# A 2048-point column transform split as 128 x 16 in place of 16 x 128, real and imaginary parts packed in one tile

## The chip, the cores and the metric

The kernel runs on one core of a Trainium2 chip. The core has five engines: TensorE (PE in the profile; its weight loads are PEld), VectorE (DVE), ScalarE (ACT), GpSimd (POOL) and SyncE (SP), which here issues DMAs. The metric is the device time of one execution in microseconds (us), as a median of runs.

## What is computed

The input x is 2048 x 640 in fp32. Two branches are mixed by a gate for each row. Cut to what matters:

```python
g = sigmoid((x * gate_w).sum(-1))                 # one number per row
# A: attention of each row to itself and 7 earlier rows, 2 apart; 32 heads of 20
q, k, v = split(x @ wqkv)                         # 640 x 1920
attn = softmax(where(idx >= 0, q.k * 20**-0.5, -1e9))
a = (attn @ v) @ wo                               # 640 x 640
# B: a filter in the frequency domain
X = rfft2(x)                                      # over 2048 rows and 640 columns
b = irfft2(X * (w_r + 1j * w_i), (2048, 640))
out = g * a + (1 - g) * b
```

The change concerns branch B alone. Its two-dimensional transform consists of a transform over the 640 columns (here: the row transform, within each row) and one over the 2048 rows (the column transform), forward and back. All of it is done with matmuls against tables of sines and cosines.

## The kernel before

**Layout.** Row s = 16 p + j of x lies in partition p of tile j, j = 0 to 15. Even j ("par 0") and odd j ("par 1") are handled apart for the attention, since a row attends only to rows of its own parity.

**The order of the work.** The program does not issue instructions as it is written. Every call is recorded by `Plan.record` (lines 174 to 190) with what it reads and writes and with a cost from `Plan.cost` (line 192 on), and `Plan.order` (lines 226 to 291) then lays out one fixed list for each engine: at each step the engine takes, of the operations that are ready by the planned times, the one with the longest chain of planned work behind it (its `tail`). Chains with a name ("logits", "sums", "even") count the rest of their own chain on an engine in that tail. All instructions of the trace therefore carry one line, L460, and are told apart by their tiles. On the chip each engine runs its list strictly in order; a SyncE DMA that waits for a buffer holds up the DMAs behind it.

**The stages** (`work`, line 392):

1. `qkv` (512), up to 237.8 us: x @ wqkv for the even rows, then the odd rows, each product split in three matmuls of a shorter fp32 format (tiles xe and xo by w). Results go to DRAM through `ev`.
2. `fold` (624) and `cols` (647), inside stage 1: each row is folded by its symmetries (f), and the matmul `z <- fc, f` does the first part of the column transform: a 16-point real transform over groups of 16 partitions (`fc` is a 128 x 128 table, eight copies of it interleaved). ScalarE copies z to `zg`, the big intermediate (128 partitions, 5 blocks, 128 positions, 16 components).
3. `attend` (550), from about 80 us to 456: for each half of four heads, VectorE forms the products pr of q and k and sums them to the logits L, GpSimd, ScalarE and VectorE do the softmax, GpSimd multiplies by v (pv, two operations at a time), VectorE sums to o (o0a to o7b), and o is stored in DRAM (od). It is spread over VectorE and GpSimd beside all other stages. The two last halves, 4a and 4b, are done in lockstep in four pieces, so that rows become complete one pair of tiles after the other.
4. `freq` (669), from 237.8 us to about 366: the rest of the transform, the filter and the way back, for one frequency kk of the 16-point transform at a time, in the order KORD (line 20), staged four deep. Seven are full (two components, real and imaginary), and kk = 0 and 8 are half (one real component). For a full one:
   - ScalarE copies its two components out of zg (`zc`, 640 elements at a stride of 16); SyncE loads the tables `md` and `mf` and the weights `wp`.
   - TensorE does the row transform: `u` and `v`, three matmuls each (widths 321, 161, 160) for each component; ScalarE copies v to `vs`; VectorE makes four sums `ab` of 321 elements.
   - TensorE does the 128-point complex column transform: `xa`, `xb` (the rows k) and `xc`, `xd` (the mirrored rows), two matmuls of 321 columns each.
   - The filter: ScalarE copies xa and xb to `X`, GpSimd multiplies by wp to `P`, twice 642 elements and then two sums; VectorE takes xc and xd straight from PSUM, with four products (`p`, and in place), two sums, and four sums of P with them to `s`, the stationary operands of the inverse.
   - The inverse column transform: `g <- mf, s`, for each of 5 blocks two matmuls of 256 columns that add up (one term from s1, one from s2). ScalarE copies g back into zg.
   A half frequency leaves out half of this; its sums run on GpSimd and ScalarE, and its g matmuls have 128 columns.
5. `project_even` (872): for each even j, the o rows are loaded (`ot`), transposed by TensorE (`oTp`), split (`oT`), multiplied by wo (`woa`, `wob`, 15 matmuls each), scaled by the gate and stored (`ad`). They have no early deadline and fill TensorE from about 300 us on.
6. `spatial` (797), 366 to 440 us: `oa`, `ob` (inverse row transform, six matmuls), copies `os`, then `ha`, `hb <- os, fct`: the last 16-point inverse. Odd j: ScalarE scales into `ho`. Even j: VectorE combines (tiles h, ha, y), GpSimd adds the even projection (yi), and the row is stored.
7. `project_odd` (888), 440 us to the end: as 5, for odd j, with the final sum on VectorE.

**Buffers around the change.** PSUM has eight banks. `freq` uses one for v, two for u, two in turn for xa to xd, one for g (line 29). In SBUF zc, md, wp, ab, P, s and X have two buffers each, vs, p and mf one (lines 374 to 376). Tags are shared between stages: the tile x7, last used by stage 1, is also the oT of `project_even` (line 379), and a later user of a tag waits for all earlier ones.

Of the kernel before, what the change touches and what calls it, by code (L numbers as in the profile page):

```python
# [16 lines left out]
S, D = 2048, 640  # L17
NJ = 16
HD = 20
KORD = (0, 8, 1, 2, 3, 4, 5, 6, 7)  # L20
# [12 lines left out]
def dft_tables():  # L33
    tau = 2 * np.pi
    ke, ko = PERM[:161], PERM[161:]
    kb = PERM[2:161]
    b = np.arange(16)
    coef = np.zeros((16, 16))
    coef[0] = 1
    coef[1] = (-1.0) ** b  # L40
    for k in range(1, 8):
        coef[2 * k] = np.cos(tau * b * k / 16)
        coef[2 * k + 1] = -np.sin(tau * b * k / 16)
    fc = np.einsum("cb,ae->baec", coef, np.eye(8)).reshape(128, 128)
# [15 lines left out]
    a = np.arange(128)  # L60
    a = 16 * (a % 8) + a // 8
    k1 = np.arange(128)
    md = np.zeros((9, 128, 384))
    mf = np.zeros((9, 128, 512))
    for kk in range(9):
        psi = tau * (np.outer(k1, a) / 128 + kk * a[None, :] / 2048)
        c, s = np.cos(psi), np.sin(psi)
        md[kk] = np.concatenate([c.T, s.T, -s.T], 1)
        mf[kk] = np.stack([np.stack([c, s], 2), np.stack([s, -c], 2)], 1).reshape(128, 512)
# [3 lines left out]
    def ck(k):  # L73
# [12 lines left out]
        "t_fc": np.concatenate([fc, fc.T], 1).astype(f),  # L86
        "t_bt": bt.astype(f),
        "t_md": md.astype(f),
        "t_mf": mf.astype(f),
# [240 lines left out]
class Mixer:  # L330
# [17 lines left out]
    def places(self, pp, dr, sb):  # L348
# [8 lines left out]
        self.ident, self.fc, self.fct = (self.one(n, 128) for n in ("ident", "fc", "fct"))  # L357
# [34 lines left out]
    def work(self):  # L392
# [25 lines left out]
        self.zg = self.one("zg", 5, 128, 16, tag="big")  # L418
# [11 lines left out]
        S.dma_start(self.fct, ins["t_fc"][:, 128:256])  # L430
# [11 lines left out]
        freq = [self.freq(kk) for kk in KORD]  # L442
# [204 lines left out]
    def cols(self, q):  # L647
        p = self.p
        f = self.folded[q]
        for t0, n in ((0, 2), (2, 2), (4, 1)):  # L650
            z = self.ps(BP, f"z{q}_{t0}")
            for i in range(2 * n):
                t, j = t0 + i // 2, i % 2
                p.pe.matmul(
                    z[:, i * 128 : i * 128 + 128],
                    f[:, j, t * 128 : t * 128 + 128],
                    self.fc,
                    start=(i == 0),
                    stop=(i == 2 * n - 1),
                    skip_group_check=True,  # L660
                )
            p.chain = "z"
            p.act.copy(
                self.zg[:, t0 : t0 + n, 16 * q : 16 * q + 16, :].rearrange("p t a c -> p t (a c)"),
                z[:, 0 : 256 * n].rearrange("p (t m) -> p t m", t=n),
            )
            p.chain = ""

    def freq(self, kk):
# [3 lines left out]
        full = kk not in (0, 8)  # L673
        comps = (2 * kk, 2 * kk + 1) if full else ((0,) if kk == 0 else (1,))
        pm = 2 if full else 1
        md, wp = self.mdr.next(f"md{kk}", 384), self.wpr.next(f"wp{kk}", 4, 321)
        S.dma_start(md, ins["t_md"][kk])
        S.dma_start(wp[:, 0 : 2 * pm], ins["ws"][kk, :, 0 : 2 * pm])

        us, vs, zcs = {}, {}, {}  # L680
        for c in comps:
            zcs[c] = self.zcr.next(f"zc{c}", 5, 128)
            A.copy(zcs[c], zg[:, :, :, c])

        def row(o, c, t, r, start, stop):
            T.matmul(o, zcs[c][:, t], r, start=start, stop=stop, skip_group_check=True)

        if full:
            vv = self.vsr.next(f"vs{kk}", 2, 321)
        for c, d in zip(comps[::-1], comps):  # L690
            v = self.ps(BV, f"v{c}")[:, 0:321]
            row(v, c, 3, bt[:, 803:1124], True, False)
            row(v[:, 0:161], c, 2, bt[:, 642:803], False, False)
            row(v[:, 161:321], c, 4, bt[:, 1124:1284], False, True)
            if full:
                A.copy(vv[:, c % 2], v)
                v = vv[:, c % 2]
            u = self.ps(BU, f"u{d}")[:, 0:321]
            row(u, d, 1, bt[:, 161:482], True, False)
            row(u[:, 0:161], d, 0, bt[:, 0:161], False, False)  # L700
            row(u[:, 161:321], d, 2, bt[:, 482:642], False, True)
            us[d], vs[c] = u, v
        us, vs = [us[c] for c in comps], [vs[c] for c in comps]

        ab = self.abr.next(f"ab{kk}", 4, 321)
        if full:
            v0, v1 = vs
            V.tensor_sub(ab[:, 0], us[0], v1)
            V.tensor_add(ab[:, 2], us[0], v1)
            V.tensor_add(ab[:, 1], us[1], v0)  # L710
            V.tensor_sub(ab[:, 3], v0, us[1])
        else:
            A.copy(ab[:, 1], vs[0])
            A.copy(ab[:, 0], us[0])

        yield
        cs, sn, ns = md[:, 0:128], md[:, 128:256], md[:, 256:384]

        def col(nm, i, sa, sb):
            o = self.ps(BX, f"{nm}{kk}")[:, 0:321]  # L720
            T.matmul(o, sa, ab[:, i], start=True, stop=False)
            T.matmul(o, sb, ab[:, i + 1], start=False, stop=True)
            return o

        x0, x1 = col("xa", 0, cs, sn), col("xb", 0, ns, cs)
        X = self.Xr.next(f"X{kk}", 2, 321)
        A.copy(X[:, 0], x0)
        A.copy(X[:, 1], x1)
        P = self.Pr.next(f"P{kk}", 4, 321)
        G.tensor_mul(P[:, 0:2], X, wp[:, 0:2])  # L730
        G.tensor_mul(P[:, 2:4], X, wp[:, 1::-1])
        if full:
            G.tensor_sub(P[:, 0], P[:, 0], P[:, 1])
            G.tensor_add(P[:, 2], P[:, 2], P[:, 3])

        yield
        mf = self.mfr.next(f"mf{kk}", 512)
        S.dma_start(mf, ins["t_mf"][kk])
        s12 = self.s12r.next(f"s{kk}", 2, 640)
        s1, s2 = s12[:, 0], s12[:, 1]  # L740
        if full:
            x2, x3 = col("xc", 2, cs, ns), col("xd", 2, sn, cs)
            t = self.p1r.next(f"p{kk}", 2, 321)
            V.tensor_mul(t[:, 0], x2, wp[:, 2])
            V.tensor_mul(x2, x2, wp[:, 3])
            V.tensor_mul(t[:, 1], x3, wp[:, 2])
            V.tensor_mul(x3, x3, wp[:, 3])
            V.tensor_sub(x3, t[:, 0], x3)
            V.tensor_add(x2, t[:, 1], x2)
            V.tensor_add(s1[:, 0:321], P[:, 0], x3)  # L750
            V.tensor_sub(s2[:, 321:640], P[:, 0, 2:], x3[:, 2:])
            V.tensor_add(s1[:, 321:640], P[:, 2, 2:], x2[:, 2:])
            V.tensor_sub(s2[:, 0:321], x2, P[:, 2])
        else:
            G.tensor_sub(s1[:, 0:321], P[:, 0], P[:, 1])
            G.tensor_sub(s2[:, 321:640], P[:, 0, 2:], P[:, 1, 2:])
            G.tensor_add(s1[:, 321:640], P[:, 2, 2:], P[:, 3, 2:])
            G.tensor_add(P[:, 0], P[:, 2], P[:, 3])
            A.mul(s2[:, 0:321], P[:, 0], -1.0)
        yield  # L760
        n = 256 if full else 128
        per = 2 if full else 4
        m1 = mf[:, 0:256] if full else mf[:, 0:256:2]
        m2 = mf[:, 256:512] if full else mf[:, 256:512:2]
        for t0 in range(0, 5, per):
            k = min(per, 5 - t0)
            g = self.ps(BG, f"g{kk}_{t0}")
            for i in range(k):
                t = t0 + i
                go = g[:, i * n : i * n + n]  # L770
                T.matmul(go, s1[:, t * 128 : t * 128 + 128], m1, start=(i == 0), stop=False, skip_group_check=True)
                T.matmul(go, s2[:, t * 128 : t * 128 + 128], m2, start=False, stop=(i == k - 1), skip_group_check=True)
            if full:
                A.copy(
                    zg[:, t0 : t0 + k, :, 2 * kk : 2 * kk + 2].rearrange("p t a r -> p (t a) r"),
                    g[:, 0 : k * n].rearrange("p (t r) -> p t r", r=2),
                )
            else:
                A.copy(zg[:, t0 : t0 + k, :, comps[0]].rearrange("p t a -> p (t a)"), g[:, 0 : k * n])
# [17 lines left out]
    def spatial(self, j):  # L797
# [21 lines left out]
        T.matmul(h1[:, 0:322], self.fct, os[:, 0:322], start=True, stop=True)  # L819
        T.matmul(h2[:, 0:322], self.fct, os[:, 322:644], start=True, stop=True)  # L820
# [117 lines left out]

def arrays_of(inputs):
# [4 lines left out]
    up = [16 * np.arange(128) + k for k in range(9)]  # L944
    down = [(2048 - r) % 2048 for r in up]
# [29 lines left out]
```

## Time and profile before

| | |
|---|---|
| median of 3 runs | 484.64 us (484.53 to 484.76) |
| profiled execution | 485.85 us, span of its instructions 484.1 us |
| TensorE, its weight loads | 474.5 us busy (98% of the span), 406.2 (84%) |
| VectorE, GpSimd, ScalarE | 405.3 (84%), 372.2 (77%), 235.2 (49%) |
| DMA moved | 101.59 MB, mean 210 GB/s |
| granted TensorE clock | 1.00 throughout |

How to read the lines that follow: a row of a group names the engine, the operation, the tile written and the tiles read ("g<-mf,s"; buffer numbers are left out), the shape and the count; then the busy time of the group and the mean ns of one; then the idle time of the engine just before these instructions and who ended it. An fp32 matmul appears as two MATMUL records with a weight load each, so 10 calls are 20 records. Rows of the chain in order of time have start, length, engine and tile, and a count of records. Rows of waits have the total in us, the number of times and the longest. Rows by stage have, behind the stretch's ends and its length, the busy time of each engine with its number of instructions, then the granted clock, the DMA share and GB/s. In a timeline a row has start and length.

### The profile page before, as it was taken

What the parts mean: (1) busy time and instruction counts of PE and PEld (TensorE: products, weight loads), DVE (VectorE), ACT (ScalarE), POOL (GpSimd) and SP (SyncE); (2) the same over time, 40 slices, a digit from 0 to 9 for tenths busy, and PEclk for the clock granted to TensorE, in tenths of its full rate; (3) what the DMA queues carried; (4) which work ended last, traced back from release to release, by engine and by line L of the source; (5) the groups of instructions that cost most, each with busy time, mean ns of one, the idle gap of its engine ahead of it and who ended that gap; (6) DMA issues with size and microseconds to landing.
All of it is one profiled execution on the core that took longest, in us unless ns stands there. A gap on an engine that the chain in (4) does not pass through costs nothing.

```text
span 484.1 us, 7137 instructions
## 1 busy us (share of the span) xinstructions
PE 474.5 (98%) x2449; PEld 406.2 (84%) x2449; DVE 405.3 (84%) x511; ACT 235.2 (49%) x474; POOL 372.2 (77%) x316
## 2 busy tenths in 40 slices
PE   8999999999999999999999999999999999998997
PEld 5888888888898898888878777888878888887996
DVE  4989789947999999896983778989999998879536
ACT  5633456733375654674496445355344755433110
POOL 1014437989999899896999777787688989799990
PEclk9999999999999999999999999999999999999999
DMA  8999999797787895987674433744544322345752
GB/s 280 401 401 317 405 301 323 214 340 194 228 264 246 245 325 145 262 235 197 222 238 125 164 108 109 245 132 137 172 118 128 89 71 73 120 159 160 255 164 82
DMA packets 77460, 101.59 MB, mean 210 GB/s; under 512 B 21344, under 2 KB 58848, under 8 KB 77424
## 3 DMA queue, kind: packets, MB, share of 16 engines
q1 hardware_dynamic: 51136, 80.91, 52.9%
q10 hardware_dynamic: 25376, 16.22, 10.8%
q0 software_dynamic: 912, 4.00, 2.0%
q8 instruction: 19, 0.31, 0.2%
q14 instruction: 17, 0.14, 0.1%
HBM read 68.28 MB, written 32.84 MB: 209 GB/s over the span
## 4 chain that ended last, share of the span: by engine, by line
PE 93%; DMA 3%; DVE 2%; ACT 1%; issue 1%; DVEq 0%
PE qkv L460 43%; PE woa L460 7%; PE wob L460 7%; PE g L460 7%; PE ob L460 4%; PE oa L460 4%; PE z L460 3%; PE v L460 3%; PE u L460 3%; PE xb L460 2%; PE ha L460 2%; PE oTp L460 2%; PE hb L460 2%; PE xa L460 2%; PE xd L460 1%; PE xc L460 1%
## 5 line engine op out<-in xcount | busy, mean ns | idle before, releaser
L460 PE MATMUL qkv<-w,xo 128*128 128x480 f32 (+1 forms) x480 | 106.2, 382 | 0.5 <-ACT zg L460 0.5
L460 PEld LDWEIGHTS qkv<-w,xo 128*128 128x128 f32 x480 | 90.2, 189 | 15.0 <-ACT zg L460 0.7
L460 PE MATMUL qkv<-w,xe 128*128 128x480 f32 (+1 forms) x465 | 102.5, 382 | 0.0
L460 PEld LDWEIGHTS qkv<-w,xe 128*128 128x128 f32 x465 | 87.6, 188 | 14.8 <-ACT w L460 0.2
L460 ACT COPY ev<-qkv 128x480 f32<-128x480 f32 x64 | 35.6, 561 | 57.7 <-PE qkv L460 39.0
L460 PE MATMUL woa<-wo,oT 128*128 128x320 f32 x240 | 54.3, 318 | 0.6 <-ACT oT L460 0.6
L460 PE MATMUL wob<-wo,oT 128*128 128x320 f32 x240 | 53.8, 316 | 0.6 <-ACT ya L460 0.6
L460 PEld LDWEIGHTS wob<-wo,oT 128*128 128x128 f32 x240 | 40.1, 188 | 1.9 <-ACT ya L460 0.9
L460 PEld LDWEIGHTS woa<-wo,oT 128*128 128x128 f32 x240 | 40.0, 188 | 1.9 <-ACT oT L460 0.8
L460 PE MATMUL g<-mf,s 128*128 128x256 f32 (+1 forms) x180 | 39.9, 359 | 0.6 <-ACT zg L460 0.4
L460 POOL TENSOR_TENSOR w<-raw,w 128x480 fp32r<-128x480 f32 (+1 forms) x20 | 25.3, 1278 | 15.4 <-ACT w L460 15.4
L460 PEld LDWEIGHTS g<-mf,s 128*128 128x128 f32 x180 | 30.7, 189 | 7.5 <-ACT zg L460 2.6
L460 POOL DMA_DIRECT2D fd<-fx x6 | 4.3, 722 | 37.2 <-DVE fx L460 35.3
L460 POOL TENSOR_TENSOR P<-X,wp 128x642 f32<-128x642 f32 x18 | 26.6, 1503 | 6.9 <-ACT X L460 6.9
L460 ACT CAST oT<-oTp 128x384 fp32r<-128x384 f32 (+1 forms) x32 | 13.1, 430 | 28.9 <-PE oTp L460 28.9
L460 DVE TENSOR_TENSOR oT<-oTp,oT 128x384 fp32r<-128x384 f32 (+1 forms) x32 | 15.0, 485 | 11.5 <-ACT oT L460 11.3
L460 ACT COPY zg<-g 128x512 f32<-128x512 f32 (+2 forms) x25 | 14.0, 560 | 19.6 <-PE g L460 19.5
L460 PE MATMUL oa<-gt,zg 128*128 128x161 f32 (+1 forms) x96 | 22.0, 344 | 0.0
L460 ACT COPY zc<-zg 128x640 f32<-128x640 f32 x16 | 20.6, 1323 | 1.2 <-PE u L460 1.2
L460 PE MATMUL v<-bt,zc 128*128 128x321 f32 (+2 forms) x96 | 20.6, 345 | 0.6 <-ACT zc L460 0.6
L460 PE MATMUL ob<-gt,zg 128*128 128x161 f32 (+1 forms) x96 | 21.0, 344 | 0.0
L460 PE MATMUL u<-bt,zc 128*128 128x321 f32 (+2 forms) x96 | 20.6, 344 | 0.0
(316 smaller groups left out, 1147.0 us busy)
## 6 DMA issues: line engine op xcount, KB each, us to landing
qkvd<-ev ACTq DMA_DIRECT2D x32, 480.0 KB, 4.6
raw<-in_wqkv SPq DMA_DIRECT2D x25, 240.0 KB, 6.1
fx<-in_x SPq DMA_DIRECT2D x8, 641.0 KB, 9.3
ot<-od SPq DMA_DIRECT2D x16, 320.0 KB, 3.1
wp<-in_ws SPq DMA_DIRECT2D x7, 642.0 KB, 4.1
fd<-fx POOLq DMA_DIRECT2D x6, 640.0 KB, 8.1
f<-fd SPq DMA_DIRECT2D x6, 640.0 KB, 5.3
xt<-in_xT SPq DMA_DIRECT2D x8, 320.0 KB, 4.0
```

The source lines that it names most:

```text
L460: p.dve.memset(w, 0.0)
```

## The change

The 2048-point column transform is split the other way round. `fc` becomes a real transform over the 128 partitions: 64 frequencies with real and imaginary part fill the 128 outputs (frequency 64, which is real, takes the place of the imaginary part of frequency 0). What remains is a 16-point complex transform over j, done for 16 groups of four of these frequencies: the 128 partitions of a group are 2 parts x 16 j x 4 frequencies. Group 0 holds the two special frequencies and has tables of its own.

- `zg` is (128, 5, 16 j, 128); `zc` is made by three ScalarE operations: 3 blocks as they are, and 3 blocks with real and imaginary parts exchanged and a sign (so that v comes out multiplied by the imaginary unit).
- u and v have three matmuls each for each of 16 groups, as they had for each of 16 components; `ab` takes two VectorE sums.
- xa, xb, xc and xd are one matmul of 321 columns each (two in group 0).
- GpSimd does one product of 642 and one sum to P; VectorE three operations on xc and xd and two to s.
- The inverse g is one matmul of 128 columns for each of 5 blocks (six in group 0), in tiles of three and two blocks.
- `wp` has 16 tiles of 4 x 321 (before: 7, and two of 2 x 321); the tables are five tiles of 3 x 320 in the place of the nine md and nine mf, and 1280 elements for group 0, in the tile x7.
- `fct` is two tables of 128 x 128, and ha and hb are two matmuls of 161 columns each, in place of one of 322.
- The order of the groups is 1, 2, 3, 0, 4 to 15. The other stages, the planner and its costs are unchanged.

The diff's core (for `freq`, the added and kept lines; the removed ones stand in the listing above; the loops that fill the sine tables of the groups are left out):

```diff
-KORD = (0, 8, 1, 2, 3, 4, 5, 6, 7)
+GORD = (1, 2, 3, 0) + tuple(range(4, 16))
...
+    pos = np.arange(128)
+    fc = np.zeros((128, 16, 2, 4))
+    for k in range(64):
+        fc[:, k // 4, 0, k % 4] = np.cos(tau * pos * k / 128)
+        fc[:, k // 4, 1, k % 4] = -np.sin(tau * pos * k / 128)
+    fc[:, 0, 1, 0] = (-1.0) ** pos
+    back = np.stack([fc, np.stack([-fc[:, :, 1], fc[:, :, 0]], 2)]).reshape(2, 128, 128)
+    fc = fc.reshape(128, 128)
...
-        self.zg = self.one("zg", 5, 128, 16, tag="big")
+        self.zg = self.one("zg", 5, NJ, 128, tag="big")
...
-    def freq(self, kk):
+    def freq(self, g):
         p, ins = self.p, self.ins
         V, A, G, T, S = p.dve, p.act, p.pool, p.pe, p.sp
         zg, bt = self.zg, self.bt
+        if g == 0:
+            tb = self.one("tbfirst", 1280, tag="x7")
+            S.dma_start(tb, ins["t_first"])
         else:
+            if g % 3 == 1:
+                self.mm = self.mdr.next(f"mm{g}", 3, 320)
+                S.dma_start(self.mm, ins["t_mm"][(g - 1) // 3])
+            tb = self.mm[:, (g - 1) % 3]
+        wp = self.wpr.next(f"wp{g}", 4, 321)
+        S.dma_start(wp, ins["ws"][g])
+        zc = self.zcr.next(f"zc{g}", 6, NJ, 8)
+        A.copy(zc[:, 0:3], zg[:, 0:3, :, 8 * g : 8 * g + 8])
+        A.mul(zc[:, 3:6, :, 0:4], zg[:, 2:5, :, 8 * g + 4 : 8 * g + 8], -1.0)
+        A.copy(zc[:, 3:6, :, 4:8], zg[:, 2:5, :, 8 * g : 8 * g + 4])
+        def row(o, t, r, start, stop):
+            T.matmul(o, zc[:, t].rearrange("p j c -> p (j c)"), r, start=start, stop=stop, skip_group_check=True)
+        v = self.ps(BV, f"v{g}")[:, 0:321]
+        row(v, 4, bt[:, 803:1124], True, False)
+        row(v[:, 0:161], 3, bt[:, 642:803], False, False)
+        row(v[:, 161:321], 5, bt[:, 1124:1284], False, True)
+        vv = self.vsr.next(f"vs{g}", 321)
+        A.copy(vv, v)
+        u = self.ps(BU, f"u{g}")[:, 0:321]
+        row(u, 1, bt[:, 161:482], True, False)
+        row(u[:, 0:161], 0, bt[:, 0:161], False, False)
+        row(u[:, 161:321], 2, bt[:, 482:642], False, True)
+        ab = self.abr.next(f"ab{g}", 2, 321)
+        V.tensor_add(ab[:, 0], u, vv)
+        V.tensor_sub(ab[:, 1], u, vv)
         yield
+        def col(nm, i, turned):
+            o = self.ps(BX, f"{nm}{g}")[:, 0:321]
+            if g == 0:
+                c = 256 * i + 128 * turned
+                T.matmul(o, tb[:, c : c + 128], ab[:, 0], start=True, stop=False)
+                T.matmul(o, tb[:, 512 + c : 640 + c], ab[:, 1], start=False, stop=True)
+            else:
+                c = 0 if turned else 64
+                T.matmul(o, tb[:, c : c + 128], ab[:, i], start=True, stop=True)
             return o
+        X = self.Xr.next(f"X{g}", 2, 321)
+        for i, nm in enumerate(("xa", "xb")):
+            A.copy(X[:, i], col(nm, 0, i))
+        P = self.Pr.next(f"P{g}", 2, 321)
+        G.tensor_mul(P, X, wp[:, 0:2])
+        G.tensor_add(P[:, 0], P[:, 0], P[:, 1])
         yield
+        z, sz = col("xc", 1, 0), col("xd", 1, 1)
+        t = self.p1r.next(f"p{g}", 321)
+        V.tensor_mul(t, z, wp[:, 2])
+        V.tensor_mul(sz, sz, wp[:, 3])
+        V.tensor_sub(sz, t, sz)
+        s = self.s12r.next(f"s{g}", 768)
+        d0 = 321
+        if g == 0:
+            d0 = 449
+            G.memset(s[:, 384:449], 0.0)
+        V.tensor_add(s[:, 0:321], P[:, 0], sz)
+        V.tensor_sub(s[:, d0 : d0 + 319], P[:, 0, 2:], sz[:, 2:])
         yield
+        last = s[:, 640:768] if g == 0 else s[:, 512:640]
+        chunks = [[(s[:, 0:128], 0)], [(s[:, 128:256], 0)], [(s[:, 256:384], 0)], [(s[:, 384:512], 1)], [(last, 1)]]
+        if g == 0:
+            chunks[2:4] = [[(s[:, 384:512], 1), (s[:, 256:321], 0)], [(s[:, 512:640], 1)]]
+        for t0, n in ((0, 3), (3, 2)):
+            o = self.ps(BG, f"g{g}_{t0}")
+            for i in range(n):
+                for w, back in chunks[t0 + i]:
+                    m = tb[:, 1024 + 128 * back : 1152 + 128 * back] if g == 0 else tb[:, 192:320]
+                    T.matmul(
+                        o[0 : w.shape[1], i * 128 : i * 128 + 128],
+                        w,
+                        m,
+                        start=(i == 0),
+                        stop=(i == n - 1),
+                        skip_group_check=True,
+                    )
+            A.copy(
+                zg[:, t0 : t0 + n, :, 8 * g : 8 * g + 8],
+                o[:, 0 : n * 128].rearrange("p (t j c) -> p t j c", t=n, c=8),
+            )
...
-            st = zg[:, t, 8 * j : 8 * j + 8, :].rearrange("p a c -> p (a c)")
-            T.matmul(o, st, r, start=start, stop=stop, skip_group_check=True)
+            T.matmul(o, zg[:, t, j], r, start=start, stop=stop, skip_group_check=True)
...
-        T.matmul(h1[:, 0:322], self.fct, os[:, 0:322], start=True, stop=True)
-        T.matmul(h2[:, 0:322], self.fct, os[:, 322:644], start=True, stop=True)
+        for i, h in enumerate((h1, h2)):
+            for a in range(2):
+                T.matmul(
+                    h[:, 161 * a : 161 * a + 161],
+                    self.fct[:, a],
+                    os[:, 322 * i + 161 * a : 322 * i + 161 * a + 161],
+                    start=(a == 0),
+                    stop=(a == 1),
+                    skip_group_check=True,
+                )
...
+def rows_of(g):
+    up = np.tile((4 * g + np.arange(4)[None] + 128 * np.arange(16)[:, None])[None], (2, 1, 1))
+    if g == 0:
+        up[:, :, 0] = [0, *range(128, 1024, 128), *range(64, 1088, 128)]
+        up[1, 0, 0] = 1024
+    down = (2048 - up) % 2048
+    return up.reshape(-1), down.reshape(-1)
```

More of the change, by code (lines that the diff above doesn't have):

```diff
@@ L58, in dft_tables @@
     )
[L60 to L69, printed above, removed]
+    j, k2 = np.arange(16), np.arange(16)
+    md = np.zeros((16, 16, 2, 4, 2, 16, 4))
@@ new lines, in dft_tables @@
+    mf = np.zeros((16, 2, 16, 4, 16, 2, 4))
+    for g in range(16):
+        for a in range(4):
+            th = tau * np.outer(j, 4 * g + a + 128 * k2) / 2048
+            c, s = np.cos(th), np.sin(th)
+            md[g, :, 0, a, 0, :, a], md[g, :, 1, a, 0, :, a] = c, s
+            md[g, :, 0, a, 1, :, a], md[g, :, 1, a, 1, :, a] = -s, c
+            mf[g, 0, :, a, :, 0, a], mf[g, 1, :, a, :, 0, a] = c.T, -s.T
+            mf[g, 0, :, a, :, 1, a], mf[g, 1, :, a, :, 1, a] = s.T, c.T
+    u0, u64, v0, v64 = (np.zeros((2, 2)) for _ in range(4))
@@ new lines, in dft_tables @@
+    first = np.zeros((2, 2, 2, 16, 2, 4, 2, 16, 4))
+    g0 = md[0].copy()
+    g0[:, :, 0] = 0
+    for x in range(2):
+        first[x, x, 0] = g0
+        first[x, x, 1, :, :, :, 0], first[x, x, 1, :, :, :, 1] = -g0[:, :, :, 1], g0[:, :, :, 0]
+    first[:, :, :, :, :, 0, :, :, 0] = one
+    first = first.reshape(8, 128, 128).transpose(1, 0, 2).reshape(128, 1024)
+    mfu, mfv = mf[0].copy(), mf[0].copy()
+    for q, w in ((mfu, mu), (mfv, mv)):
+        q[:, :, 0] = 0
+        q[:, :, 0, :, :, 0] = w
@@ L85, in dft_tables @@
     return {
[L86 removed]
+        "t_fc": np.concatenate([fc, back[0].T, back[1].T], 1).astype(f),
         "t_bt": bt.astype(f),
[L88 to L89 removed]
+        "t_mm": mm.reshape(5, 3, 128, 320).transpose(0, 2, 1, 3).astype(f),
+        "t_first": first.astype(f),
         "t_gt": gt.astype(f),
@@ L356, in places @@
         self.a_d = dr.tile([128, 8, D], F32, tag="dram_a", name="ad")
-        self.ident, self.fc, self.fct = (self.one(n, 128) for n in ("ident", "fc", "fct"))
+        self.ident, self.fc = (self.one(n, 128) for n in ("ident", "fc"))
+        self.fct = self.one("fct", 2, 128)
         self.z, self.g, self.ng, self.nng = (self.one(n, NJ) for n in ("z", "g", "ng", "nng"))
@@ L672, in freq @@
         zg, bt = self.zg, self.bt
[L673 to L702, printed above, removed]
@@ L719, in col @@
[L719 to L722, printed above, removed]
-            return o
[L725 to L731, printed above, removed]
@@ L952, in arrays_of @@
         "wo": wo.reshape(5, 128, D),
-        "ws": np.stack([np.stack([w[r][:, PERM] for r in (up[k], down[k]) for w in (wr, wi)], 1) for k in range(9)]),
+        "ws": np.stack([np.stack([w[r][:, PERM] for r in rows_of(g) for w in (wr, wi)], 1) for g in range(16)]),
     }
```

97 lines of the change are left out of this document (28 added, 69 removed).

## The prediction

> **What bounds the kernel now.** First the page: busy times and the engines of the chain that ended last.
>
> ```profile
> span 484.1 us, 7137 instructions
> ...
> PE 474.5 (98%) x2449; PEld 406.2 (84%) x2449; DVE 405.3 (84%) x511; ACT 235.2 (49%) x474; POOL 372.2 (77%) x316
> ...
> PE 93%; DMA 3%; DVE 2%; ACT 1%; issue 1%; DVEq 0%
> ```
>
> TensorE is busy for 98% of the span and 93% of the final chain. The whole is an average, so next come the busy times by stage: frequency groups (237.8 to about 366), spatial transform and even projections (to 440), odd projections (to the end). A first row holds the columns; the last row, from a second question, runs to the moment at which the first pieces of the last attention halves (4a, 4b) exist.
>
> ```profile
> core 0: us, PE busy (x) PEld busy (x) DVE busy (x) ACT busy (x) POOL busy (x), PEclk, DMA share, GB/s
> 237.80:297.00 59.20, 58.11 (x285) 46.07 (x285) 40.84 (x69) 35.19 (x64) 50.07 (x46) 1.00 0.54 170
> 297.00:412.00 115.00, 113.85 (x610) 96.50 (x609) 108.53 (x134) 60.16 (x124) 96.03 (x74) 1.00 0.42 125
> 412.00:440.00 28.00, 27.70 (x148) 22.68 (x146) 24.29 (x51) 11.52 (x28) 25.35 (x21) 1.00 0.40 126
> 440.00:484.10 44.10, 39.70 (x278) 38.99 (x276) 26.46 (x53) 6.22 (x16) 29.88 (x36) 1.00 0.55 178
> ...
> 237.80:427.90 190.10, 187.86 (x983) 156.26 (x983) 161.94 (x228) 102.28 (x202) 159.35 (x132) 1.00 0.46 140
> ```
>
> Two things stand here. From 237.8 to 440, TensorE is idle for only 2.5 us (1.09 + 1.15 + 0.30), so work taken from it there should shorten the span. But VectorE is close behind: 108.53 of 115 us from 297 to 412, because the attention runs beside the transforms. If TensorE gets shorter, VectorE may become the bound. So I make two sums, one for each engine.
>
> **TensorE's sum.** An fp32 matmul shows as two records. Their spacing is the price, not their duration (records overlap), and the chain in order of time gives it: start, length, records.
>
> ```profile
> 138.90 4.46 PE z L460 x40
> 237.80 1.09 PE v L460 x6
> 272.25 1.73 PE g L460 x8
> 273.98 1.08 PE xc L460 x4
> 324.33 2.20 PE woa L460 x15
> 370.59 0.54 PE ha L460 x2
> 383.43 0.55 PE ob L460 x4
> ```
>
> A record takes 0.1115 us at 128 columns (z), 0.1375 at 161 (ob), 0.216 at 256 (g), 0.27 at 321 (xc, ha). Now the counts.
>
> ```profile
> L460 PE MATMUL g<-mf,s 128*128 128x256 f32 x140 | 34.5, 382 | 0.5 <-ACT zg L460 0.4 <-issue 0.2
> L460 PE MATMUL g<-mf,s 128*128 128x128 f32 x40 | 5.5, 277 | 0.1
> L460 PE MATMUL xa<-ab,md 128*128 128x321 f32 x36 | 11.8, 440 | 0.0
> L460 PE MATMUL xc<-ab,md 128*128 128x321 f32 x28 | 9.2, 433 | 0.0
> ```
>
> *Inverse (g).* Before: 140 records of 256 columns and 40 of 128, 140 x 0.216 + 40 x 0.1115 = 34.7 us. After: 16 groups of 5 matmuls and one extra for group 0, 81 matmuls or 162 records of 128 columns: 18.1 us. Saved: 16.7. This is "the inverse in one term": real and imaginary parts fill the 128 partitions, so one matmul does what two did. *Forward columns (xa to xd).* Before: 2 x 36 + 2 x 28 = 128 records. After: 15 groups of 4 matmuls and group 0 with 8, 68 matmuls, 136 records: +8 x 0.27 = +2.2 us. *ha and hb.* 32 matmuls of 322 columns become 64 of 161: 128 x 0.1375 - 64 x 0.27 = +0.3 us. *Rows (u, v) and z* keep their number and widths: nothing. Net: -14.2 us. All these widths are priced by rows above; none is extrapolated.
>
> The change also adds weight loads: 180 + 128 + 64 = 372 before, 162 + 136 + 128 = 426 after, 54 more. The z row shows that one load per 128-column record hides: its 0.1115 us is the streaming rate of the 256-column row, halved (0.108), plus 0.0035. So I charge nothing more. The Trainium skill (Perfetto Trace Analysis, "Identifying the Most-Contended Engine") speaks against this reading: it says to judge TensorE by the busy share of weight loads and not by that of matmuls, and that share (84%) would rise here. What this would give is a rival below.
>
> **VectorE's sum, and the other engines.**
>
> ```profile
> L460 DVE TENSOR_TENSOR p<-xd,wp 128x321 f32<-128x321 f32 x7 | 3.4, 492 | 5.5 <-PE xd L460 5.3
> L460 POOL TENSOR_TENSOR P<-X,wp 128x642 f32<-128x642 f32 x18 | 26.6, 1503 | 6.9 <-ACT X L460 6.9
> L460 POOL TENSOR_TENSOR P<-P 128x321 f32<-128x321 f32 x16 | 11.8, 758 | 0.2
> L460 POOL TENSOR_TENSOR s<-P 128x319 f32<-128x319 f32 x4 | 3.0, 750 | 0.0
> L460 ACT COPY zc<-zg 128x640 f32<-128x640 f32 x16 | 20.6, 1323 | 1.2 <-PE u L460 1.2
> L460 ACT COPY X<-xb 128x321 f32<-128x321 f32 x9 | 3.9, 429 | 6.7 <-PE xb L460 6.6
> wp<-in_ws SPq DMA_DIRECT2D x7, 642.0 KB, 4.1
> ```
>
> *VectorE.* Before: 14 operations of about 321 elements in each of seven full frequencies, none in the other two: 98. After: 7 in each of 16 groups: 112. The 14 more cost 14 x 0.48 = +6.7 us (the row: 0.49, the second term of s a little less). *GpSimd.* Before: 18 x 1.50 + 16 x 0.76 + 6 x 0.75 (four in the row, two of 321) = 43.7. After: 16 x (1.50 + 0.76) = 36.2 and one small memset (under 0.75, the nearest row): -7. *ScalarE.* zc's one strided copy of 640 becomes three of 384, 192 and 192 in runs of 8 or 4 elements. At the strided price of 2.07 ns an element, the 768 elements cost 1.6 us a group, 25.4 in all; at the price of the X copy (1.34 ns) 1.0, 16.4. So -4 to +5 beside 20.6. The v and X copies go from 14 and 18, with four copies to ab, to 16 and 32: +12 x 0.43 = 5. ScalarE has half its time free: on the path, nothing. *DMA.* 16 weight tiles of 642 KB take the place of seven and two halves, eight more, in all some 4 MB with the smaller tables; at a DMA share of about 0.5 I charge nothing while the second buffer of wp (4.1 us to land) covers it. The SP queue issues 22 loads for the groups where it issued 27; each wp waits there for VectorE's last use of the buffer two groups back, with the attention's loads and stores behind it. That wait existed; it now comes 14 times in place of 7, and what it costs is in the bounds below, through the attention.
>
> What decides is when the last attention halves are far enough for the odd projections. The timelines of VectorE and of TensorE, then the landing times of o4b's stores and of ot's loads:
>
> ```profile
> 426.41 1.49 DVE L460 TENSOR_REDUCE o4b<-pv4b 128x160 f32<-128x1280 f32 x1 [2.53 <-POOL pv4b L460]
> ```
>
> ```profile
> 437.83 0.38 PE L460 MATMUL oTp<-ident,ot 128*128 128x128 f32 x2
> ```
>
> ```profile
> DMA to landing us min/median/max: 1.7/2.1/5.4
> ```
>
> ```profile
> DMA to landing us min/median/max: 2.9/3.1/5.2
> ```
>
> The first piece of o4b ends at 427.9, is stored 2.1 us later and loaded 3.1 after that, at 433.1 or, with the two hand-overs, some 5.3 us after its end (an estimate); TensorE takes it up at 437.8. With 14.2 us less it would want it at 423.6, so the piece must end by 418.3. Up to 427.9 VectorE had 161.94 us of work and 28.2 idle. After, the work is 168.6, and 237.8 + 168.6 = 406.4: only 11.9 us of idle time fit. Will so much idle time go? VectorE's longest waits from 237.8 to 440:
>
> ```profile
> DVE p L460 <- PE xd L460: 5.3, 4, 1.9
> DVE p L460 <- PE xc L460: 4.5, 4, 1.9
> DVE ab L460 <- ACT s L460: 4.0, 1, 4.0
> DVE ab L460 <- PE u L460: 2.2, 2, 1.3
> DVE L6a L460 <- POOL pv3b L460: 2.1, 1, 2.1
> ```
>
> These 18.1 us fall at the start of the frequency stage, where (first two rows of the stages) VectorE had 69% and GpSimd 85%. There the two half frequencies gave VectorE nothing and GpSimd much (2 x 1.50 + 0.76 + 3 x 0.75, 6 us each), and a full one came only every 13 us. Sixteen equal groups feed VectorE from the start and leave GpSimd 7 us for the attention. I take half of the 18.1 as gone: idle 19.1. VectorE also did this much of the even rows' last step before 427.9 (tile h, in the same window):
>
> ```profile
> 237.80:427.90 190.10, 7.12 (x19) 2.12 (x4) 1.00 0.46 140
> ```
>
> Half of that 7.1 can move behind the pieces of o4, since the stage after 440 leaves VectorE 17.6 us idle: 3.6. The piece then ends at 406.4 + 19.1 - 3.6 = 421.9, 3.6 us late. Both halves are my choice, midway between none and all.
>
> The sum: the profiled execution took 485.85 us (span 484.1 and 1.75 around it), 1.2 over the median of 484.64. 485.85 - 14.2 + 3.6 = 475.25 profiled, **474.0** as a median.
>
> **The rivals.**
>
> *TensorE alone decides.* Idle falls to 11.9 or late steps move wholly: 484.64 - 14.2 = 470.4, 469.5 if some of TensorE's own 2.5 us go too. For it: the list order puts the longer tail first, and can hold back even rows. Against: VectorE would need 93% from 237.8 to 418.3, as it had only from 297 on.
>
> *The banks of xa to xd pace the first groups.* xb, its copy, xd, and xd's last use after P take 0.54 + 0.43 + 0.54 + 0.97, and P 2.26 beside xd: about 4.2 us through one PSUM bank, where TensorE's work for a group is 5.45 (2.17 rows, 2.16 columns, 1.12 inverse). The new waits are VectorE's on xc, xd and P, with attention reductions queued behind. With one more GpSimd operation of 1.5 and one reduction of 1.5 ahead, a group takes 7.2. From group 4 on, even projections (two blocks of 2.2 like woa's, 4.4 each) fill the gaps; before, they can't, since their oT lies in x7, where the change puts group 0's tables. Four groups x 1.75 = 7 us: 481.
>
> *Slower: the attention is not helped.* If VectorE's idle stays at 28.2 and nothing moves, the first piece ends at 434.6, 16.3 late: 486.7. It is slower from an idle of 26.1 on (11.9 + 14.2). For it: VectorE gets 6.7 us more and the attention's chain through both engines is unchanged. Against: GpSimd's 7 us less, and waits that belonged to the half frequencies.
>
> *Weight loads bind after all.* Then 54 more loads cost 54 x 0.1115 = 6 us and no narrower stream pays: 490.7. By the trend of the skill's measure it would come out so. The z row speaks against it, since there loads and streams of 128 columns run one for one at streaming speed.
>
> *It doesn't do what it says* (more stalls eat just the 14): 484.6.
>
> **How the numbers follow.** Forecast (471.5 to 478) 0.52; TensorE alone 0.18; banks (478 to 483.5) 0.17; no change 0.03; attention not helped 0.08; loads 0.02. The range 469.5 to 483 takes the first three. A measurement of this kernel can tell 0.2% (about 1 us) from no change: faster 0.87, same 0.03, slower 0.10.
>
> **What would show it.** Right: 162 records of g at spacing 0.11, TensorE busy near 460, first odd oTp near 427, VectorE above 80% from 237.8 to 297, its total near 412. Wrong: g's records spaced much above 0.11 (loads), TensorE idle for over 7 us before the fourth group's inverse with xb or xc waiting for s or X (banks), or o4's first pieces after 430 with TensorE waiting for ot (attention).

## The result and the profile after

The changed kernel takes **471.4 us** (median of 4 runs, 470.99 to 474.59) beside 484.7 us for the kernel before (4 runs, 484.53 to 485.71). The ratio is 0.9736, with an interval from 0.9691 to 0.978: 2.6% faster, 13.3 us by the medians. The forecast was 474.0, the range 469.5 to 483. The profiled execution took 470.99 us. Two executions of later kernels ran at a granted clock of 0.654 and 0.754 and took 663.95 and 578.82 us; no ratio below contains them.

First its page: span, busy times, engines of the chain that ended last.

```profile
span 469.1 us, 7335 instructions
...
PE 458.2 (98%) x2503; PEld 401.1 (85%) x2503; DVE 411.6 (88%) x525; ACT 234.5 (50%) x523; POOL 366.7 (78%) x309
...
PE 83%; POOL 8%; DVE 6%; DMA 1%; issue 1%; ACT 0%; DVEq 0%; POOLq 0%
```

TensorE's busy time fell by 16.3 us (its ends are modelled), VectorE's rose by 6.3 and GpSimd's fell by 5.5. The chain, which was 93% TensorE, now has 14% of GpSimd and VectorE in it. GpSimd's part lies in one place: in order of time, from

```profile
405.02 2.99 POOL pv4a L510 x2
...
446.53 0.76 POOL y L510
```

the chain runs through GpSimd with no more than short gaps (the two longest are 1.0 and 1.4 us). Next the busy times by stage, with the same two starts as before (237.8 and 297), then a stretch in which GpSimd is never idle, then the stretch up to the first piece of o4b, and in that stretch the work on tile h alone:

```profile
core 0: us, PE busy (x) PEld busy (x) DVE busy (x) ACT busy (x) POOL busy (x), PEclk, DMA share, GB/s
237.80:297.00 59.20, 59.20 (x325) 48.58 (x324) 56.09 (x95) 38.55 (x100) 51.52 (x43) 1.00 0.67 221
297.00:412.00 115.00, 112.43 (x698) 100.30 (x697) 110.96 (x149) 63.03 (x146) 96.43 (x76) 1.00 0.42 132
412.00:426.00 14.00, 12.84 (x79) 10.79 (x78) 11.67 (x24) 5.71 (x13) 14.00 (x10) 1.00 0.56 184
...
237.80:416.10 178.30, 175.73 (x1044) 152.49 (x1043) 169.54 (x247) 102.94 (x249) 152.05 (x120) 1.00 0.51 164
...
237.80:416.10 178.30, 9.45 (x25) 2.65 (x5) 1.00 0.51 164
```

The largest move is not TensorE's. In the first 59.2 us VectorE went from 40.84 busy to 56.09, from 69% to 95%. Up to the first piece of o4b it now works 169.54 us and is idle for 178.30 - 169.54 = 8.8, where it was idle for 28.2. Its waits from 230 to 430 (total, times, longest) show where that went:

```profile
DVE y L510 <- DMA ad<-ya: 1.6, 1, 1.6
DVE oT L510 <- ACT oT L510: 1.2, 3, 0.6
DVE p L510 <- PE xc L510: 1.1, 4, 0.3
...
DVE ab L510 <- PE u L510: 0.4, 2, 0.2
```

The waits for xc and xd were 9.8 us; for xc 1.1 is left, and xd's is no longer among the leading rows. The wait of ab for s (4.0) is gone too, and so is one of before that lay directly ahead of the first piece, for GpSimd's pv4b:

```profile
DVE o4b L460 <- POOL pv4b L460: 2.5, 1, 2.5
```

Next, the groups that the change touches (count, busy time, mean ns of one, idle time before them):

```profile
L510 PE MATMUL g<-mm,s 128*128 128x128 f32 x150 | 22.8, 276 | 2.5 <-DVE s L510 2.5
L510 PE MATMUL ha<-os,fct 128*128 128x161 f32 x64 | 13.7, 301 | 0.5 <-DVE y L510 0.5
L510 POOL TENSOR_TENSOR P<-X,wp 128x642 f32<-128x642 f32 x16 | 24.9, 1556 | 14.3 <-ACT X L510 8.0 <-DVE o7b L510 6.2
L510 ACT COPY zc<-zg 128x384 f32<-128x384 f32 x16 | 8.2, 513 | 0.0
L510 ACT ACTIVATE zc<-zg 128x192 f32<-128x192 f32 x16 | 5.9, 366 | 4.9 <-PE u L510 4.5
L510 ACT COPY zc<-zg 128x192 f32<-128x192 f32 x16 | 5.4, 340 | 0.0
```

The inverse has its 162 records: 150 here and 12 that read group 0's table. Their spacing is in the chain in order of time:

```profile
265.64 0.66 PE g L510 x6
270.67 0.67 PE g L510 x6
```

That is 0.111 us a record, as priced. Last, the timelines of VectorE and of TensorE at the point that decides:

```profile
414.62 1.48 DVE L510 TENSOR_REDUCE o4b<-pv4b 128x160 f32<-128x1280 f32 x1
...
423.07 0.38 PE L510 MATMUL oTp<-ident,ot 128*128 128x128 f32 x2
```

The first piece of o4b ends at 416.1, 2.2 us before the 418.3 that TensorE needed, and the first odd projection starts at 423.07 where TensorE's sum wanted it at 423.6. Part of this was there before the changed stages began. The first v, before and after:

```profile
237.64 1.25 PE L460 MATMUL v<-bt,zc 128*128 128x321 f32 x6
236.13 1.25 PE L510 MATMUL v<-bt,zc 128*128 128x321 f32 x6
```

The 1.5 us between them vary from execution to execution: kernels below that keep these same lists start it between 236.4 and 237.7. Counted from there, the first odd projection came 13.25 us earlier, close to the 13.3 of the medians.

### The profile page after: what moved, and what is told of

It reads as the page before. It is cut to its first block, busy times and chain, and to the rows that moved or that the text cites. A ratio compares the mean times of both kernels' runs of the same rounds, so it can differ in the third digit from the quotient of the medians.

```text
span 469.1 us, 7335 instructions
## 1 busy us (share of the span) xinstructions
PE 458.2 (98%) x2503; PEld 401.1 (85%) x2503; DVE 411.6 (88%) x525; ACT 234.5 (50%) x523; POOL 366.7 (78%) x309
## 4 chain that ended last, share of the span: by engine, by line
PE 83%; POOL 8%; DVE 6%; DMA 1%; issue 1%; ACT 0%; DVEq 0%; POOLq 0%
PE qkv L510 45%; PE wob L510 5%; PE woa L510 4%; PE v L510 4%; PE u L510 4%; PE g L510 4%; PE z L510 3%; POOL pv4a L510 3%; POOL pv4b L510 2%; PE xb L510 2%; PE xa L510 2%; PE oa L510 2%; PE xd L510 2%; PE xc L510 2%; POOL yi L510 2%; PE ob L510 2%
## 5 line engine op out<-in xcount | busy, mean ns | idle before, releaser
L510 PE MATMUL woa<-wo,oT 128*128 128x320 f32 x240 | 47.9, 317 | 0.0
L510 PE MATMUL wob<-wo,oT 128*128 128x320 f32 x240 | 47.4, 316 | 0.2 <-DVE y L510 0.2
L510 PEld LDWEIGHTS wob<-wo,oT 128*128 128x128 f32 x240 | 38.0, 188 | 1.0 <-DVE y L510 0.4
L510 PEld LDWEIGHTS woa<-wo,oT 128*128 128x128 f32 x240 | 38.2, 188 | 0.8 <-ACT oT L510 0.2
L510 POOL TENSOR_TENSOR P<-X,wp 128x642 f32<-128x642 f32 x16 | 24.9, 1556 | 14.3 <-ACT X L510 8.0
L510 PEld LDWEIGHTS g<-mm,s 128*128 128x128 f32 x150 | 21.1, 190 | 5.6 <-ACT vt5b L510 1.8
L510 PE MATMUL g<-mm,s 128*128 128x128 f32 x150 | 22.8, 276 | 2.5 <-DVE s L510 2.5
L510 DVE TENSOR_TENSOR oT<-oTp,oT 128x384 fp32r<-128x384 f32 (+1 forms) x32 | 15.2, 485 | 10.4 <-ACT oT L510 10.2
L510 PEld LDWEIGHTS v<-bt,zc 128*128 128x128 f32 x96 | 16.5, 189 | 4.9
L510 PE MATMUL u<-bt,zc 128*128 128x321 f32 (+2 forms) x96 | 20.6, 344 | 0.0
L510 PE MATMUL ob<-gt,zg 128*128 128x161 f32 (+1 forms) x96 | 20.6, 344 | 0.0
L510 ACT CAST w<-raw 128x480 fp32r<-128x480 f32 (+1 forms) x30 | 17.1, 596 | 4.5 <-DMA raw<-in_wqkv 3.1
## 6 DMA issues: line engine op xcount, KB each, us to landing
fx<-in_x SPq DMA_DIRECT2D x8, 641.0 KB, 10.2
```

The lines of the kernel that those rows point to most:

```text
L510: p.dve.memset(w, 0.0)
```

## The experiments

The first theory was the prediction's: TensorE's shorter work sets the time as long as VectorE follows. The rivals were weight loads that bind, VectorE or GpSimd as the true bound, and, after the first runs, the lists themselves: each edit makes the planner draw new lists for every engine, and new lists may cost by themselves. So the later kernels keep the lists: the planner records the operation of the kernel it started from, and only at issue is that operation left out or replaced. The table gives the ratio to the kernel before in the same batch of runs, with its interval. The last column is the difference between that ratio and the one of the kernel edited (1 for the kernel before, 0.9736 for the changed one), times 484.7 us. The 0.9736 itself is known to some 2 us.

| edit | lists | ratio | interval | against the kernel edited, us |
|---|---|---|---|---|
| before, inverse in one term | new | 0.996 | 0.9933 to 0.9987 | -1.9 |
| the same | kept | 0.9875 | 0.9858 to 0.9891 | -6.1 |
| one term, GpSimd less | new | 0.9897 | 0.9843 to 0.9951 | -5.0 |
| the same | kept | 0.9899 | 0.9869 to 0.9929 | -4.9 |
| before, ha and hb split | new | 1.0116 | 1.0097 to 1.0135 | +5.6 |
| the same | kept | 1.0001 | 0.9979 to 1.0023 | 0.0 |
| changed, fewer row matmuls | new | 0.9862 | 0.9841 to 0.9883 | +6.1 |
| the same | kept | 0.9663 | 0.9631 to 0.9696 | -3.5 |
| changed, inverse twice | kept | 1.0056 | 1.0038 to 1.0075 | +15.5 |
| changed, more GpSimd work | new | 0.9857 | 0.9835 to 0.988 | +5.9 |
| changed, more VectorE work | new | 0.9918 | 0.9889 to 0.9947 | +8.8 |
| changed, other planner settings | new | 0.9866 | 0.9845 to 0.9886 | +6.3 |

**The inverse's TensorE saving alone, in the kernel before.**

```diff
-                T.matmul(go, s2[...], m2, start=False, stop=(i == k - 1), ...)
+                if not full:
+                    T.matmul(go, s2[...], m2, start=False, stop=end, ...)
```

> The kernel before, with the second term (s2) of the inverse left out in the seven full frequencies: 35 matmuls of 256 columns, 70 records x 0.216 = 15.1 us less for TensorE, while VectorE and GpSimd keep all their work and the half frequencies. (The result then lacks that term.) Theory A, TensorE sets the pace and VectorE's idle time before was only slack: 484.7 - 15.1 = 469.6 us. Theory B, the step of the forecast, that VectorE's idle time goes only where the new layout takes its causes away: the first piece of o4b would have to end at 437.8 - 15.1 - 5.3 = 417.4, which leaves 17.7 us for 28.2 of idle time, so 10.5 late, about 480.

With new lists it gains 1.9 us. With the lists of before kept:

> As e1 (the kernel before without the inverse's second term in the full frequencies, 15.1 us of TensorE), with every list as in the kernel before. (The result lacks that term.) Theory A, TensorE alone: 15.1 below the kernel before, ratio 0.969. Theory B, the attention on VectorE and GpSimd sets the pace too: their work is unchanged; only VectorE's 9.8 us of waits for xc and xd can go, and at most the 5 us go that the first piece of o4b lay ahead of its use: ratio 0.99 or above.

It gains 6.1 of the 15.1 us taken away. The ratio of 0.9875 lies just below the second theory's 0.99 and far from the first's 0.969. The windows, and VectorE's waits from 237 to 431, of the kernel with the lists kept:

```profile
237.80:297.00 59.20, 56.99 (x276) 43.60 (x275) 42.73 (x73) 36.67 (x66) 51.79 (x48) 1.00 0.53 167
237.80:421.60 183.80, 175.44 (x907) 141.13 (x906) 160.09 (x227) 101.35 (x201) 158.13 (x131) 1.00 0.47 143
```

```profile
DVE p L463 <- PE xd L463: 4.3, 4, 1.7
DVE ab L463 <- ACT s L463: 4.0, 1, 4.0
DVE p L463 <- PE xc L463: 3.1, 2, 2.1
```

VectorE stays at 72% in the first stretch and idle for 23.7 us up to the first piece of o4b. Its waits are still there, and TensorE now has 2.2 us of idle time in that stretch itself. Less TensorE work, in an order that leaves VectorE waiting, pays 40%. The kept order was planned for the longer TensorE work; with lists planned for the shorter work the gain is no larger, 1.9 us, or 5.3 if the 3.4 us of halved clock in its trace are put back (an estimate; the clock is taken up below).

**GpSimd's relief added to it.** Half of GpSimd's second product is left out as well, in all nine frequencies, and the sums read P[:, 1] in its place.

```diff
-        G.tensor_mul(P[:, 2:4], X, wp[:, 1::-1])
+        G.tensor_mul(P[:, 2], X[:, 0], wp[:, 1])
```

> As e1 (the kernel before without the inverse's second term), and with GpSimd's second product halved to 321 elements in all nine frequencies: 9 x (1.50 - 0.76) = 6.7 us less for GpSimd. (The result lacks that term and uses a wrong product.) Theory B, the attention runs through GpSimd and sets the pace: some 6.7 below e1, 476.5. If GpSimd's work doesn't matter: 483, as e1.

> As e9, with GpSimd's second product halved as in e7 (9 x 0.75 = 6.7 us less for GpSimd) and still every list as in the kernel before. (The result lacks the term and uses a wrong product.) If GpSimd's share of the attention's chain sets the pace: up to 6.7 us below e9. If VectorE's own list does, no change from e9.

With the lists kept it gives no more than the one term alone (-4.9 beside -6.1, the intervals overlap). The first stretch answers why:

```profile
237.80:297.00 59.20, 56.98 (x278) 43.85 (x278) 42.88 (x73) 36.34 (x67) 49.88 (x49) 1.00 0.53 171
```

GpSimd is busy for 1.9 us less there (4.1 over the whole span: the products take 5.8 less, and nine of the sums 0.11 more each) and VectorE does 0.15 us more. In this order VectorE's waits for GpSimd are few and don't shrink: 2.1 us for pv3b in the first stretch and 2.5 for pv4b ahead of the first piece, with GpSimd's relief and without. With new lists the total is the same -5.0; that kernel's trace isn't read here.

**More weight loads.** ha and hb in two halves of 161 columns, as in the change, but in the kernel before: 64 more loads and the same streams.

```diff
-        T.matmul(h1[:, 0:322], self.fct, os[:, 0:322], start=True, stop=True)
-        T.matmul(h2[:, 0:322], self.fct, os[:, 322:644], start=True, stop=True)
+        for i, h in enumerate((h1, h2)):
+            for a in range(2):
+                T.matmul(h[:, 161 * a : 161 * a + 161], self.fct,
+                         os[:, 322 * i + 161 * a : 322 * i + 161 * a + 161], ...)
```

> The kernel before, with ha and hb each made by two matmuls of 161 columns in place of one of 322, and nothing else: 64 more records and weight loads at the same number of columns. If weight loads hide: 128 x 0.1375 - 64 x 0.27 = +0.3 us, 485.0. If weight loads bind: 64 x 0.1115 = +7.1 us, 491.8.

The +5.6 us looked like loads that bind. With the lists kept:

> As e2 (the kernel before with ha and hb in two matmuls of 161 columns each), with every list as in the kernel before. If e2's +5.5 us came from the new order of the lists: +0.3, 485.0 by the earlier median, ratio 1.001. If it came from the 64 more weight loads: ratio 1.011 again.

```profile
PE 474.2 (98%) x2513; PEld 411.5 (85%) x2513; DVE 405.2 (84%) x511; ACT 234.3 (48%) x474; POOL 371.8 (77%) x316
```

The weight loads are busy for 5.3 us more (406.2 before) and the time is the same to 0.2%. To within some 1 us the loads hide, where 64 at 0.1115 us would have cost 7.1, and the +5.6 were the new lists.

**Less TensorE work in the changed kernel.** The side matmuls of u and v are left out, 17.4 us (shown for u; v is changed likewise).

```diff
...
-        row(u, 1, bt[:, 161:482], True, False)
-        row(u[:, 0:161], 0, bt[:, 0:161], False, False)
-        row(u[:, 161:321], 2, bt[:, 482:642], False, True)
+        row(u, 1, bt[:, 161:482], True, True)
```

> The changed kernel without the side matmuls (widths 161 and 160) of u and v: 64 matmuls, 128 records x 0.136 = 17.4 us less for TensorE. (Most of the row transform is then missing.) It asks where the next bound lies. TensorE still alone: 471.4 - 17.4 = 454.0. VectorE next: it had 178.3 - 169.5 = 8.8 us idle from 237.8 to the first piece of o4b at 416.1, and TensorE took the rows 1.7 us after they were there, so at most 10.5 go: 460.9 or more.

It is 6.1 us slower than the changed kernel, with 17.4 us less to do. TensorE's timeline and the windows (PEclk is the third column from the end) at one of three places show a reason:

```profile
346.18 0.69 PE L510 MATMUL oTp<-ident,ot 128*128 128x128 f32 x2 [2.17 <-DVE oT L510]
```

```profile
340.00:344.00 4.00, 2.67 (x12) 1.55 (x10) 4.00 (x5) 1.18 (x3) 3.06 (x3) 1.00 0.35 127
344.00:348.00 4.00, 1.83 (x10) 1.65 (x9) 3.57 (x10) 0.69 (x2) 4.00 (x5) 0.68 0.47 127
348.00:352.00 4.00, 4.00 (x17) 4.00 (x16) 3.96 (x5) 0.48 (x1) 2.84 (x3) 0.50 0.27 78
352.00:356.00 4.00, 4.00 (x27) 3.68 (x26) 4.00 (x4) 2.64 (x7) 1.89 (x2) 0.97 0.00 0
```

After a pause of 2.17 us TensorE's granted clock is halved. These rows lose 4 x (0.32 + 0.50 + 0.03) = 3.4 us of full clock. The same happens near 246 and near 428, after pauses of 1.99 and 2.34. Three times 3.4 us is 10.2. The kernel with the lists kept, whose clock is 1.00 throughout those stretches, is 9.7 us faster; how much of that is the clock and how much the order isn't separated:

> As e3 (the changed kernel without the side matmuls of u and v, 17.4 us of TensorE), but every engine keeps the list of the changed kernel, with the matmuls left out at issue. (Most of the row transform is missing.) Theory A, TensorE alone sets the pace: 454.0 us. Theory B, VectorE and GpSimd with the attention set it too: their lists are unchanged and had 8.8 us idle on VectorE up to the first piece of o4b; at most 10.5 go, 461 or more. If e3's 479 was the attention itself and not its list, this one is near it too; if e3 was a bad list, it is at or below 471.

```profile
237.80:415.20 177.40, 165.33 (x924) 134.78 (x923) 170.19 (x248) 102.50 (x251) 153.59 (x123) 1.00 0.53 168
```

Of 17.4 us only 3.5 are gained. VectorE is 96% busy up to the first piece of o4b, at 415.2 where it was 416.1, while TensorE has 12 us of idle time in the stretch. The engines of its final chain:

```profile
PE 58%; DVE 21%; POOL 12%; issue 3%; DMA 3%; ACT 1%; POOLq 0%; DVEq 0%; ACTq 0%
```

In the changed kernel VectorE is a bound too, and by the chain GpSimd after it.

**TensorE's saving put back.** Every matmul of the inverse is issued twice in the changed kernel, +18.1 us.

```diff
+                    def twice(to, w, m, start, stop):
+                        T.real.matmul(to, w, m, start=start, stop=False, ...)
+                        T.real.matmul(to, w, m, start=False, stop=stop, ...)
```

> The changed kernel with every g matmul made twice, one behind the other, and every list unchanged: 81 more matmuls, 162 records x 0.1115 = 18.1 us for TensorE, which is what the one-term inverse took away and a little more. (The result doubles the inverse.) If only VectorE and GpSimd set the pace, little change: 471 to 475. If TensorE is as full as they are, its idle time of about 5 us up to the odd projections is all that absorbs it: 471.4 + 18.1 - 5 = 484 or more.

The time rises by 15.5 us and lies above that of the kernel before. In the first stretch TensorE has no idle time and VectorE waits for it again, 8.8 us for xc alone from 230 to 440:

```profile
237.80:297.00 59.20, 59.20 (x352) 49.65 (x351) 49.05 (x85) 34.42 (x89) 47.41 (x42) 1.00 0.60 194
```

```profile
DVE p L510 <- PE xc L510: 8.8, 8, 1.7
```

**More work on GpSimd, and on VectorE.** A second P sum in ten groups (GpSimd's total rises by 7.1 us), and p's first product twice in each group (VectorE's by 6.6).

```diff
+        if g in GORD[:10]:
+            G.tensor_add(P[:, 1], P[:, 0], P[:, 1])
```

```diff
         V.tensor_mul(t, z, wp[:, 2])
+        V.tensor_mul(t, z, wp[:, 2])
```

> The changed kernel, with one more sum of 321 elements on GpSimd (into the half of P that nobody reads any more) in the first ten groups: 10 x 0.75 = 7.5 us, which gives back what the change saved there. TensorE alone: no change, 471.4. If the relief of GpSimd was what let the attention keep up (it is busy without a gap from 405 to 426 in the changed kernel, and 8% of its final chain): up to 7.5 longer, 478.9.

> The changed kernel with VectorE's first product on xc made twice, in all 16 groups: 16 x 0.40 = 6.4 us more for VectorE. Theory A: no change, 471.4. Theory B: up to 6.4 more, 477.8, as e4 did with GpSimd (7.5 us more there, about 7 us longer).

They cost 5.9 and 8.8 us, but both have new lists, and both have halved stretches of the clock in the windows: one of 1.7 us in the first, 1.7 and 3.4 in the second. What is left, 4.2 and 3.7, is about what new lists cost the split kernel beside its clock (5.6 - 1.7 = 3.9), so these two runs decide nothing.

**Other lists, same arithmetic.** The changed kernel with another bias of the planner and other pieces of the odd rows on GpSimd.

```diff
-BIAS = {}
+BIAS = {"": 3.0}
-ODD_POOL = (1, 3, 5, 7, 9, 11)
+ODD_POOL = (5, 7, 9, 11)
```

> The changed kernel with other lists: the operations without a chain name (transforms, inverse, odd projections) get 3 us more priority against the attention, and GpSimd leaves the final combination of rows 1 and 3 to VectorE (some 5 us of work each way, in the last stage). If the pace is set by how VectorE's list alternates between groups and attention, the time moves by more than the work does, either way (466 to 477); if only the amount of work counts, it stays within 1 us of 471.4.

It is 6.3 us slower with the same arithmetic, at full clock throughout the stages compared. In the first stretch:

```profile
237.80:297.00 59.20, 57.12 (x306) 45.93 (x306) 54.12 (x94) 37.34 (x99) 52.83 (x46) 1.00 0.68 210
```

TensorE loses 2.1 us here, and the first piece of o4b starts at 420.6 instead of 414.6. That isn't the lists alone. VectorE is busy for 11.0 us more in all (422.6 beside 411.6), as it took over sums from GpSimd, and the first of them lie ahead of that piece:

```profile
415.37 2.99 DVE L510 TENSOR_TENSOR ye<-ho 128x322 f32<-128x322 f32 x2
```

So up to 3.0 of the 6.0 us at the piece are moved work. The kernel is still 1.3% faster than the kernel before (0.9845 to 0.9886). No kernel with the whole computation was faster than the changed one.

## Why the prediction was right, point by point

**TensorE's sum: right.** 162 records of g took 0.111 us each, as priced. Busy time is 458.2 where the text said near 460. That this saving was needed is shown by putting it back: +18.1 us of matmuls cost 15.5.

**Weight loads: right.** The split of ha and hb alone, lists kept, costs nothing that can be told from the noise (1.0001, interval 0.9979 to 1.0023). The Trainium skill (Perfetto Trace Analysis, "Identifying the Most-Contended Engine") takes the busy share of weight loads, beside the share of peak arithmetic, for the measure of TensorE's room, and not the busy share of matmuls. Here that share went from 84% to 85% both in the split kernel and in the changed one, and foretold neither time. In the split kernel the loads' busy time rose by 5.3 us and the time stayed; in the changed one it fell from 406.2 to 401.1 us with 54 loads more, and the share rose only because the span is shorter.

**VectorE's and GpSimd's work: right in size.** VectorE needed 169.5 us up to the first piece of o4b where 168.6 were forecast, and its total is 411.6 where the text said near 412. GpSimd's P operations cost 1.56 us each instead of 1.50. zc's three copies take 8.2 + 5.9 + 5.4 = 19.5 us, inside the bounds of -4 to +5 around 20.6.

**The step that was mis-sized: VectorE's idle time.** "I take half of the 18.1 as gone: idle 19.1." The trace has 8.8. Idle time fell by 19.4, more than the whole 18.1: of the waits listed 1.5 are left (xc 1.1, u 0.4), and the prediction's list leaves out two waits as long as its last rows, 2.5 for pv4b and 2.3 for oT. VectorE begins at 95% where 69% stood. That this comes with the layout and not with TensorE's saving is shown by two runs: 72% with the saving alone, and 83% (49.05 of 59.2) in the changed kernel with its inverse doubled. Whether another place for the half frequencies in the order of the kernel before would have done it too wasn't tried. The other half-step, "half of that 7.1 can move behind the pieces of o4", didn't happen: 9.45 us of tile h lie before the first piece, 2.3 more than before. The two errors point in opposite ways. Forecast up to the piece: 168.6 - 3.6 = 165.0 of work and 19.1 idle, 184.1. Measured: 169.5 and 8.8, 178.3. Work was 4.5 us too low, mostly because nothing moved, and idle time 10.3 too high; together that is the 5.8 us between 421.9 and 416.1, of which 1.5 are the earlier start of the stage in this execution. So the piece wasn't 3.6 us late, nothing was given back, and the first odd projection came at 423.07, not near 427. The time fell inside the range because this term was small; the mechanism behind the forecast's last 3.6 us did not occur.

**The rival that came nearest, "TensorE alone decides" (470.4, given 0.18), came true in its own terms.** It asked that VectorE's idle time fall to 11.9, and it fell to 8.8; the doubt named against it, that VectorE would need 93%, was met with 95%. Its name says too much, though. If TensorE alone decided, 17.4 us less work on it would give far more than 3.5, and 15.1 less in the lists of before far more than 6.1. What the runs show is that two things had to change together. TensorE's work alone gives 6.1 us, while VectorE goes on waiting at the start of the stage, where the half frequencies stand. The equal groups without TensorE's saving give nothing: the changed kernel with the inverse doubled, 18.1 - 14.2 = 3.9 us above TensorE's sum of before, takes 1.0056 of its time. Together they give 13.3, and then both engines are full (TensorE 98.6% and VectorE 95% of the stretch to the first piece).

**GpSimd's 7 us: open.** I named them as what the attention would gain from. Leaving 6.7 us out by count (4.1 by busy time) in the lists of before gained nothing. But the changed kernel's chain runs through GpSimd from 405.0 to 446.5 or so, where the chain of before had no GpSimd in it, and the one run with more GpSimd work there has new lists. So whether the relief matters in the changed kernel isn't shown.

**The banks of xa to xd: absent.** TensorE is busy for all of the 59.2 us where that rival wanted stalls.

**What the prediction didn't weigh: the lists.** New lists alone moved the time by 5.6 us (ha and hb split, with 1.7 us of clock lost), 9.7 (fewer rows, with 10.2 lost), 4.1 (one term, with 3.4 lost in one halved stretch after a pause of 3.14 us) and 0.1 (GpSimd less); other settings, with some work moved, by 6.3. A change that leads to new lists carries an uncertainty of that size beside its sum. No kernel with the whole computation beat the changed one, so the list it drew may have been a lucky one, and how much of the 13.3 us is that list stays open; the changed work in the lists of before wasn't tried, since the operations don't correspond one to one.

## What to carry to other kernels

A final chain that is 93% one engine does not say that the gain is that engine's: add up work and idle time of the second engine up to the moment at which its result is wanted, and ask which of its waits the change removes. Where a planner orders the instructions, an experiment that changes one cost must keep the order, or it measures the new order; of four edits run both ways here, three gave another answer once the order was kept. Look at the granted clock of each stretch before a slower run is put down to the edit.

## What of the hardware was not expected

Pauses of TensorE from 1.85 us on were mostly followed by a halved clock, for stretches of two lengths. In the kernels with new lists the granted clock fell to 0.50 after pauses of 1.85, 1.99, 2.17, 2.19, 2.34, 2.78 and 3.14 us, and each time the windows add up to a loss of 1.7 or 3.4 us of full clock. After the pauses between 1.2 and 1.71 us it didn't fall; once, in the split kernel, it fell after one of 1.10, and two pauses of 1.94 and 2.04 us there passed without it, so the length of the pause alone doesn't decide. The Trainium skill (TensorE: Matmul & The Clock Gate, "HAM oscillation — how this bites in real kernels") asks for no idle gaps above about 3.4 us; the trace differs, since the four pauses of 2.17 to 2.78 us were each followed by a fall. The changed kernel's longest pause in these stages is 1.63 us, not far below those. One of its four runs took 474.59 us at a mean clock of 0.995; it has no trace, so whether a pause halved the clock there is open.

Copies in short runs cost ScalarE little: zc's 384 elements in runs of 8 took 513 ns, 1.34 ns an element, the price of the contiguous X copy (429 ns for 321), where the strided copy before (stride 16) took 2.07.
